# MoE 1's rational function from completed squares, a shorter bias table, a later flag, and two-bank QK products in every block, in a new order

## The chip, the cores and the metric

The kernel runs on one core of one Trainium2 chip. The metric is device microseconds of one execution, the median of several. The core's engines run their own instruction streams and wait for each other on semaphores: TensorE (PE, with its weight loads as PEld), VectorE (DVE), ScalarE (ACT), GpSimd (POOL) and SyncE (SP, which here only issues DMA).

## What is computed

Attention over 2 batches, 8 heads, 768 positions with a local window and a few global positions, then two MoE-like layers over 1536 tokens. Cut to what matters:

```python
scores = q @ k.T / sqrt(64) + bias          # bias = -slope[h] * dist, -1e9 outside window and globals
x  = softmax(scores) @ v                    # (1536, 512) after the heads are put side by side
h  = x @ w_in                               # MoE 1: 512 -> 2048
P  = a[0] + a[1]*h + a[2]*h**2 + a[3]*h**3
Q  = 1.0 + abs(b[0])*abs(h) + abs(b[1])*h**2
y  = (P / (Q + 1e-6)) @ w_out               # 2048 -> 512
h2 = y @ w2_in                              # MoE 2: 512 -> 1024
s  = h2 * softmax(h2)
out = ((s - mean(s)) / sqrt(var(s) + 1e-6) * g_ln) @ w2_out
```

The weights come in 64-bit floats and are made into 32-bit ones on the chip. Each 32-bit operand of a large product is then split into a high and a low part, and a product is the sum of three.

## The kernel before, in words

The tokens stand in four blocks of 384. Three things are interleaved.

*Attention* goes by units, 48 in all (one tile of 128 positions, one pair of heads). A unit's work: two loads on SP; QK (`qk`, L459, PE); scores plus bias and their extreme (`smax`, L464, DVE); exp (L471, ACT); reciprocal (L476, L477, DVE); normalizing (L482, on DVE for the units in `NDVE`, else on POOL); transposes (L502, PE), copy (L514, ACT), PV (L509, PE), and the result's high and low part (L516 ACT, L99 DVE). A unit whose tile is the first of its batch has 128 keys, any other 256. QK has two forms: over one PSUM bank, two products with all 128 rows of the array, or over two banks, two products with 64 rows each. The first block uses two banks (the pair `h` that MoE 1 uses later), blocks 1 and 2 use one bank of the pair `s`, and block 3 (`TWO`) uses both of `s`.

*MoE 1* goes by 64 steps (a block and a slice of 128 of the 2048 columns; block 0 in two parts). Each has three groups of products into one of two banks `h` (L634, L636, L640), the rational function (`e_ops`: c L660, ch L662, abs L663, ch2 L664, sq L666, q L667, ln L669, ex L670, n1 L671, n2 L673, n3 L675, high part L677, low part L99 on POOL), and, three steps later in the list, the products with w_out (`y_mm`, L725, L726, L731).

*Weights* (48 tiles) are loaded on SP, made 32 bits wide (L565 ACT; L569 and L570, or L582 on POOL and L586; then L574, DVE), copied as high part (L604, ACT), and the low part is a subtraction by the helper `minus` (L99), on DVE for the tiles whose number is in `WDVE`, else on POOL.

*MoE 2* goes by 12 tiles of 128 tokens after MoE 1: transposes, products `h2` (L810 to L812), a softmax and normalization (`p2_soft`), transposes (L872), products with w2_out (L894 to L896).

A planner (`Plan`) lists every operation with an estimated duration, gives out banks and buffers, and emits the instructions in the order in which its own clock would start them. `UW`, `WS`, `M2` say at which step units and weights are listed; `LEADS` shifts the due times of kinds of operations; `ZS`, `NDVE` and `WDVE` choose engines. The order on each engine is fixed by that when the program is built. While the first 30 us last, small products with the identity (`fill`, L337) are put where the planner sees PE idle.

At the start, two small tensors (`ni`: the window sizes, `abt`: the six coefficients) are loaded on SP, turned into numbers (`scalars`), a distance table is made on DVE (`bias_keep`, L401 to L413) and scaled for each head on ACT (`bias_pair`, L417). A flag on DVE (L1187 to L1193) tells whether another path has to run instead.

## Time and profile before

| | us |
|---|---|
| median of three runs | 559.76 (558.61 to 561.55) |
| span of the profiled execution | 556.3 |
| PE busy | 531.8 (96%) |
| DVE busy | 446.0 (80%) |
| ACT busy | 393.0 (71%) |
| POOL busy | 182.5 (33%) |

The median stands 3.5 us above the span of the profiled execution. The granted PE clock shows 9 tenths or more in every slice of the page. A busy PE is not a PE at its peak here: products overlap, and the view counts the union of their spans, so time lost between two products shows less than it is. The start of one product to the start of the next says more.

### The profile page before, as it was taken

To read this page: it belongs to the slowest core of one execution; us is meant where nothing else is said; L and a number is where in the kernel's file an instruction comes from. 1 tells how busy PE (TensorE), PEld (TensorE's weight loads), DVE (VectorE), ACT (ScalarE), POOL (GpSimd) and SP (SyncE) were. 2 spreads that over 40 slices of the span, in tenths; PEclk is the share of its full clock that TensorE was granted. 3 is DMA by queue.
4 is the path that set the end of the run, shared out by engine and by line. 5 is a ranking of instruction groups with operands and counts; after the bars stand their busy time and mean duration, and the time that the engine had idled before them with its cause. 6 is when DMAs were issued, how large, how long until landed. Compare 5 with 4: busy or idle time off the path is not lost.

```text
span 556.3 us, 8937 instructions
## 1 busy us (share of the span) xinstructions
PE 531.8 (96%) x2910; PEld 437.0 (79%) x2910; DVE 446.0 (80%) x1104; ACT 393.0 (71%) x911; POOL 182.5 (33%) x212
## 2 busy tenths in 40 slices
...
GB/s 252 130 201 341 195 219 86 185 135 153 104 182 154 151 96 98 73 48 48 1 38 114 133 77 75 77 180 87 57 20 38 39 38 58 20 19 20 19 39 43
DMA packets 28278, 56.24 MB, mean 101 GB/s; under 512 B 3520, under 2 KB 11968, under 8 KB 28224
## 3 DMA queue, kind: packets, MB, share of 16 engines
...
q8 instruction: 25, 0.41, 0.3%
...
q10 hardware_dynamic: 144, 0.00, 0.0%
HBM read 47.72 MB, written 7.86 MB: 100 GB/s over the span
## 4 chain that ended last, share of the span: by engine, by line
PE 55%; DVE 29%; ACT 10%; issue 4%; DMA 1%; POOL 0%; SPq 0%; ACTq 0%; DVEq 0%; POOLq 0%
PE pb L894 4%; PE pb L896 4%; PE pb L895 4%; PE pb L634 4%; PE pb L810 4%; PE pb L812 4%; PE pb L811 4%; PE pb L640 4%; PE pb L731 3%; PE pb L636 3%; PE pb L725 3%; DVE t L667 3%; PE pb L459 3%; DVE wst L574 3%; PE pb L726 3%
## 5 line engine op out<-in xcount | busy, mean ns | idle before, releaser
L99 POOL TENSOR_TENSOR g<-t,g 128x384 fp32r<-128x384 f32 x64 | 69.2, 1082 | 103.9 <-ACT g L677 91.7
L634 PE MATMUL pb<-x,w 128*128 128x384 f32 x256 | 89.3, 349 | 1.8 <-DVE t L667 1.8
L636 PE MATMUL pb<-x,w 128*128 128x384 f32 x256 | 86.1, 336 | 0.0
L725 PE MATMUL pb<-w,g 128*128 128x512 f32 x192 | 77.5, 404 | 4.2 <-ACT g L677 4.2
L726 PE MATMUL pb<-w,g 128*128 128x512 f32 x192 | 75.6, 394 | 0.5 <-POOL w L99 0.5
L99 POOL TENSOR_TENSOR w<-wst,w 128x512 fp32r<-128x512 f32 x42 | 57.2, 1364 | 42.7 <-ACT w L604 38.8
L640 PE MATMUL pb<-x,w 128*128 128x384 f32 x256 | 58.0, 347 | 0.1
L731 PE MATMUL pb<-w,g 128*128 128x512 f32 x192 | 57.7, 409 | 0.2 <-POOL g L99 0.2
L634 PEld LDWEIGHTS pb<-x,w 128*128 128x128 f32 x256 | 48.1, 188 | 8.6 <-DVE t L667 4.4
L471 ACT ACTIVATE e<-e,st 128x256 f32<-128x256 f32 (+1 forms) x96 | 46.3, 486 | 6.4 <-DVE st L464 6.4
L640 PEld LDWEIGHTS pb<-x,w 128*128 128x128 f32 x256 | 44.5, 188 | 7.1 <-issue 3.1
L636 PEld LDWEIGHTS pb<-x,w 128*128 128x128 f32 x256 | 48.1, 188 | 1.5
L725 PEld LDWEIGHTS pb<-w,g 128*128 128x128 f32 x192 | 36.0, 187 | 14.4 <-ACT g L677 7.3
L660 ACT ACTIVATE t<-pb,coef 128x384 f32<-128x384 f32 x64 | 42.7, 668 | 6.1 <-PE pb L640 6.1
L482 POOL TENSOR_SCALAR e<-e,st 128x256 f32<-128x256 f32 (+1 forms) x58 | 28.0, 495 | 54.4 <-DVE st L477 48.4
L669 ACT ACTIVATE t<-t,coef 128x384 f32<-128x384 f32 x64 | 39.6, 618 | 6.8 <-DVE t L667 6.6
L662 DVE TENSOR_TENSOR t<-t,pb 128x384 f32<-128x384 f32 x64 | 35.2, 549 | 11.1 <-ACT t L663 6.5
L677 ACT CAST g<-t 128x384 fp32r<-128x384 f32 x64 | 32.8, 512 | 16.0 <-DVE t L675 15.3
L880 ACT CAST lh<-pb 128x512 fp32r<-128x512 f32 x24 | 13.9, 592 | 42.5 <-PE pb L872 42.5
L459 PE MATMUL pb<-qk 64*128 64x256 f32 (+3 forms) x192 | 41.3, 393 | 2.7 <-DVE st L464 1.0
L667 DVE SCALAR_TENSOR_TENSOR t<-pb,coef,t 128x384 f32<-128x384 f32 x64 | 39.2, 613 | 5.2 <-ACT pb L666 4.8
L671 DVE SCALAR_TENSOR_TENSOR t<-t,t 128x384 f32<-128x384 f32 x64 | 40.6, 634 | 1.3 <-ACT t L670 1.3
(113 smaller groups left out, 1293.2 us busy)
## 6 DMA issues: line engine op xcount, KB each, us to landing
...
```

The lines of the kernel that those rows point to most:

```text
L99: eng.tensor_tensor(out=out, in0=a, in1=hi.bitcast(F32), op=ALU.subtract)
L459: pe.matmul(out=score(h), lhsT=a[r, h * 128:(h + 1) * 128], rhs=a[r, 256:256 + w], start=True, stop=True)
L471: act.activation(out=e[:, h, 0:w], in_=e[:, h, 0:w], func=AF.Exp, scale=-1.0, bias=st[:, h:h + 1], accum_out=st[:, 2 + 2 * h:3 + 2 * h])
L634: pe.matmul(out=pb[:, g.h.slot, 0:n], lhsT=wt[wh.slot][:, cs[p]], rhs=xt[x[p][0].slot][:, 0:n], start=(p == 0), stop=False)
L636: pe.matmul(out=pb[:, g.h.slot, 0:n], lhsT=wt[wl.slot][:, cs[p]], rhs=xt[x[p][0].slot][:, 0:n], start=False, stop=False)
L640: pe.matmul(out=pb[:, g.h.slot, 0:n], lhsT=wt[wh.slot][:, cs[p]], rhs=xt[x[p][1].slot][:, 0:n], start=False, stop=(p == 3))
L660: op("ACT", 0.2 + 0.46 * k, lambda: act.activation(out=T(g.c), in_=h(), func=AF.Identity, scale=coef[:, 3:4], bias=coef[:, 2:3]), r=[g.h], ...
L667: op("DVE", 0.2 + 0.41 * k, lambda: stt_(out=T(g.a), in0=h(), scalar=coef[:, 5:6], in1=T(g.b), op0=ALU.mult, op1=ALU.add), r=[g.h, g.b], n ...
L671: op("DVE", 0.15 + 0.41 * k, lambda: stt_(out=T(g.a), in0=T(g.a), scalar=1.0 + 1e-6, in1=T(g.b), op0=ALU.add, op1=ALU.mult), r=[g.b], w=[g ...
L725: pe.matmul(out=pb[:, y[i].slot, :], lhsT=gt[g.gh.slot][:, c], rhs=wt[wh.slot], start=g.first, stop=False)
L726: pe.matmul(out=pb[:, y[i].slot, :], lhsT=gt[g.gh.slot][:, c], rhs=wt[wl.slot], start=False, stop=False)
L731: pe.matmul(out=pb[:, y[i].slot, :], lhsT=gt[g.gl.slot][:, c], rhs=wt[wh.slot], start=False, stop=g.last)
```

## The change

What it does, part by part.

1. *Completed squares.* With r = sqrt|a3| and the sign s of a3 (of the negated coefficients), P/s is written as h * ((r*h + m)^2 + d) + e, and Q - 1 as b * (b + k) with b = sqrt|b1| * |h|. So c becomes one Square on ACT with scale and bias, and the operation ch on DVE and sq on ACT go; q reads b twice instead of h squared in PSUM. The sign is multiplied in where y leaves PSUM. The eight scalars for that (`poly`) are made once, with four small operations on ACT and seventeen on DVE, at the start.
2. *Bias table.* It is now made of five operations on DVE (a threshold by is_ge times a large number, then max and min) in the place of nine, and it no longer needs `scalars`; `abt` is loaded on ACT's queue.
3. *Flag.* The numbers for it, and new conditions on the size of the coefficients, stand in the class `Flag`: 24 small operations on DVE behind the last step of MoE 1.
4. *QK.* Every unit has a form of its own by a string: h (both banks `h`), s (one bank `s`), t (both `s`), m (one `h` and one `s`). 12 are h in the first block; of blocks 1 and 2, 22 are m, one h, one s; block 3 has t and m.
5. *Order anew.* New `UW`, `WS`, `M2`, `ZS`, `NDVE`, `WDVE`, `LEADS`. `WDVE` has 25 tiles in the place of 6, `NDVE` 16 units in the place of 19. There are 29 fillers in the place of 51.

The core of the diff:

```diff
-UW = {1: (0, 7), 2: (8, 15), 3: (25, 14)}
+UW = {1: (0, 5), 2: (4, 15), 3: (25, 10)}
-WS = (8, 14)
-M2 = (41, 17)
+WS = (4, 4)
+M2 = (39, 5)
-START = ('hh',)
-TWO = (3,)
+QK = 'hhhhhhhhhhhhmmmmmmmmmmmmmhmmmmmmsmmmttttttmttttt'
+BANKS_OF = {"h": "hh", "s": "s", "t": "ss", "m": "hs"}
-NDVE, WDVE = (3, 4, 5, 6, 7, 8, 9, 10, 11, 14, 15, 36, 38, 39, 40, 41, 42, 44, 46), (11, 20, 31, 42, 44, 45)
+NDVE = (0, 4, 6, 8, 9, 10, 14, 23, 24, 26, 27, 31, 38, 41, 42, 47)
+WDVE = (0, 1, 5, 8, 10, 13, 15, 16, 17, 18, 19, 20, 22, 25, 26, 29, 31, 32, 34, 37, 39, 40, 41, 45, 47)
-FILL = (30.0, 0.45, 0.25)
+FILL = (30.0, 0.45, 0.4)
...
     def bias_keep():
-        dve.tensor_scalar(out=kp, in0=rel, scalar1=nl, scalar2=None, op0=ALU.is_lt)
-        dve.scalar_tensor_tensor(out=dz, in0=rel, scalar=nl, in1=rel, op0=ALU.is_lt, op1=ALU.mult)
...
-        dve.tensor_scalar(out=kp, in0=kp, scalar1=-1.0, scalar2=MASK * 256, op0=ALU.add, op1=ALU.mult)
-        dve.tensor_tensor(out=dz, in0=dz, in1=kp, op=ALU.add)
+        nf = flag.nf
+        dve.tensor_copy(nf, flag.ni)
+        nl = nf[:, 1, 0:1]
+        far, gk = -MASK * 256, kp[:, 136:144]
+        dve.tensor_scalar(out=kp, in0=rel, scalar1=nl, scalar2=far, op0=ALU.is_ge, op1=ALU.mult)
+        dve.tensor_scalar(out=gk, in0=rel[:, 136:144], scalar1=nf[:, 0, 0:1], scalar2=far, op0=ALU.is_ge, op1=ALU.mult)
+        dve.tensor_tensor(out=dz, in0=rel, in1=kp, op=ALU.max)
+        dve.tensor_scalar(out=dz[:, 136:144], in0=gk, scalar1=nl, scalar2=None, op0=ALU.max)
+        dve.tensor_tensor(out=dz[:, 0:8], in0=dz[:, 0:8], in1=dz[:, 136:144], op=ALU.min)
...
+    op("ACT", 0.85, poly_roots, r=[vab], new=[vpoly], tag="poly")
+    op("DVE", 1.8, poly_scalars, w=[vpoly], tag="poly")
...
-        op("ACT", 0.2 + 0.46 * k, lambda: act.activation(out=T(g.c), in_=h(), func=AF.Identity, scale=coef[:, 3:4], bias=coef[:, 2:3]),
-           r=[g.h], new=[g.c], tag="c")
-        op("DVE", 0.14 + 0.41 * k, lambda: dve.tensor_tensor(out=T(g.c), in0=T(g.c), in1=h(), op=ALU.mult), r=[g.h], w=[g.c], tag="ch")
-        op("ACT", 0.15 + 0.42 * k, lambda: act.activation(out=T(g.b), in_=h(), func=AF.Abs, scale=coef[:, 4:5]), r=[g.h], new=[g.b], tag="abs")
-        op("DVE", 0.2 + 0.41 * k, lambda: stt_(out=T(g.c), in0=T(g.c), scalar=coef[:, 1:2], in1=h(), op0=ALU.add, op1=ALU.mult),
+        op("ACT", 0.2 + 0.46 * k, lambda: act.activation(out=T(g.c), in_=h(), func=AF.Square, scale=poly[:, 0:1], bias=poly[:, 1:2]),
+           r=[g.h, vpoly], new=[g.c], tag="c")
+        op("ACT", 0.15 + 0.42 * k, lambda: act.activation(out=T(g.b), in_=h(), func=AF.Abs, scale=poly[:, 4:5]), r=[g.h, vpoly], new=[g.b], tag="abs")
+        op("DVE", 0.2 + 0.41 * k, lambda: stt_(out=T(g.c), in0=T(g.c), scalar=poly[:, 2:3], in1=h(), op0=ALU.add, op1=ALU.mult),
            r=[g.h], w=[g.c], occ=0.12 + 0.41 * k, tag="ch2")
-        op("ACT", 0.1 + 0.38 * k, lambda: act.activation(out=h(), in_=h(), func=AF.Square), w=[g.h], tag="sq")
-        op("DVE", 0.2 + 0.41 * k, lambda: stt_(out=T(g.a), in0=h(), scalar=coef[:, 5:6], in1=T(g.b), op0=ALU.mult, op1=ALU.add),
-           r=[g.h, g.b], new=[g.a], occ=0.12 + 0.41 * k, tag="q")
+        op("DVE", 0.2 + 0.43 * k, lambda: stt_(out=T(g.a), in0=T(g.b), scalar=poly[:, 5:6], in1=T(g.b), op0=ALU.add, op1=ALU.mult),
+           r=[g.b], new=[g.a], lock=True, tag="q")
...
+    vflag = Val()
+    for part_ in (flag.numbers, flag.factors):
+        op("DVE", 1.0, part_, r=[vnn, vpoly], w=[vflag], after=[gs[-1].op], tag="flag")
...
-    nc.sync.dma_start(out=abt, in_=ab.partition_broadcast(128))
+    nc.scalar.dma_start(out=abt, in_=ab.partition_broadcast(128))
```

What the new order makes of it, at three places, all on DVE (`t` are the buffers of the rational function, `wst` those of the weights, `pb` is PSUM, `e` and `st` belong to a unit's softmax). First, two steps of MoE 1 behind the attention, before:

```order
L662 TENSOR_TENSOR t_164<-t_164,pb 128x384
L664 SCALAR_TENSOR_TENSOR t_164<-t_164,coef,pb 128x384
L671 SCALAR_TENSOR_TENSOR t_163<-t_163,t_162 128x384
L673 SCALAR_TENSOR_TENSOR t_162<-t_163,t_162 128x384
L675 SCALAR_TENSOR_TENSOR t_160<-t_160,coef,t_162 128x384
L667 SCALAR_TENSOR_TENSOR t_166<-pb,coef,t_168 128x384
L671 SCALAR_TENSOR_TENSOR t_161<-t_161,t_165 128x384
L574 SCALAR_TENSOR_TENSOR wst_156<-wst_156,pb 128x512
L662 TENSOR_TENSOR t_163<-t_163,pb 128x384
L673 SCALAR_TENSOR_TENSOR t_165<-t_161,t_165 128x384
L675 SCALAR_TENSOR_TENSOR t_167<-t_167,coef,t_165 128x384
```

and in the changed kernel, a few steps earlier:

```order
L735 SCALAR_TENSOR_TENSOR t_158<-t_158,poly,pb 128x384
L741 SCALAR_TENSOR_TENSOR t_164<-t_164,t_162 128x384
L737 SCALAR_TENSOR_TENSOR t_161<-t_160,poly 128x384
L743 SCALAR_TENSOR_TENSOR t_162<-t_164,t_162 128x384
L745 SCALAR_TENSOR_TENSOR t_159<-t_159,poly,t_162 128x384
L737 SCALAR_TENSOR_TENSOR t_164<-t_157,poly 128x384
L735 SCALAR_TENSOR_TENSOR t_163<-t_163,poly,pb 128x384
L741 SCALAR_TENSOR_TENSOR t_161<-t_161,t_160 128x384
L741 SCALAR_TENSOR_TENSOR t_164<-t_164,t_157 128x384
L743 SCALAR_TENSOR_TENSOR t_160<-t_161,t_160 128x384
L745 SCALAR_TENSOR_TENSOR t_158<-t_158,poly,t_160 128x384
```

L662 has no successor, and L667's, L737, reads buffer t alone and no PSUM.

Second, DVE's start before, from the coefficients on (five more bias operations follow):

```order
L1181 TENSOR_SCALAR coef<-abt 128x4
L401 TENSOR_SCALAR t_161<-t_163,nv 128x264
L402 SCALAR_TENSOR_TENSOR t_160<-t_163,nv 128x264
L1187 TENSOR_SCALAR fl<-nv 128x1
L1188 TENSOR_SCALAR fl<-nv 128x1
L404 TENSOR_SCALAR t_161<-t_163,nv 128x8
L1189 TENSOR_TENSOR fl<-fl 128x1
L406 TENSOR_SCALAR t_160<-t_161,nv 128x8
```

and in the changed kernel, from the last of the first three units' maxima (L536):

```order
L536 ISA e_210,st_215<-pb,bt_198 128x128
L536 ISA st_215 128x1
L473 TENSOR_SCALAR coef<-abt 128x4
L475 RECIPROCAL root<-root 128x2
L476 TENSOR_TENSOR root<-root 128x2
L477 TENSOR_TENSOR root<-root 128x2
L478 TENSOR_SCALAR root<-root 128x2
L479 RECIPROCAL root<-root 128x2
```

The coefficients (`coef<-abt`) stood ahead of the bias table; now they stand behind the maxima, and with them sixteen operations on `root` and `poly`, ahead of the first reciprocal of a softmax.

Third, DVE behind ch2 of MoE 1's last step, before:

```order
L667 SCALAR_TENSOR_TENSOR t_161<-pb,coef,t_165 128x384
L673 SCALAR_TENSOR_TENSOR t_162<-t_163,t_162 128x384
L675 SCALAR_TENSOR_TENSOR t_160<-t_160,coef,t_162 128x384
L671 SCALAR_TENSOR_TENSOR t_161<-t_161,t_165 128x384
L673 SCALAR_TENSOR_TENSOR t_165<-t_161,t_165 128x384
L832 TENSOR_REDUCE st_2940<-pb 128x1
L833 TENSOR_SCALAR st_2940<-st_2940 128x1
L675 SCALAR_TENSOR_TENSOR t_167<-t_167,coef,t_165 128x384
L99 TENSOR_TENSOR w_115<-wst_156,w_113 128x512
```

and in the changed kernel, from the last operations of the flag:

```order
L109 TENSOR_SCALAR fl<-am 128x1
L110 TENSOR_TENSOR fl<-fl 128x1
L111 TENSOR_SCALAR fl<-am 128x1
L112 TENSOR_TENSOR fl<-fl 128x1
L113 CAST fi<-fl 128x1
L745 SCALAR_TENSOR_TENSOR t_163<-t_163,poly,t_157 128x384
L741 SCALAR_TENSOR_TENSOR t_159<-t_159,t_165 128x384
L133 TENSOR_TENSOR w_115<-wst_155,w_116 128x512
L743 SCALAR_TENSOR_TENSOR t_165<-t_159,t_165 128x384
```

Between that ch2 and these rows stand, in the changed kernel, n3 of an earlier step, n1, q, n2, the low part of MoE 2's first input, three weight joins with two more weight operations, and the flag's first nineteen operations; of the last two n3 (L745) one stands here and one follows.

## Rows read from the trace of the kernel before

**Rows 1.** Busy time by stretch: start:end, then PE, PEld, DVE, ACT, POOL busy, clock, DMA share, GB/s.

```profile
46.00:196.00 150.00, 142.83 (x817) 115.58 (x816) 143.14 (x352) 134.38 (x324) 83.88 (x100) 1.00 0.52 168
196.00:284.00 88.00, 87.84 (x511) 69.92 (x511) 74.47 (x200) 70.39 (x170) 23.65 (x27) 1.00 0.19 59
284.00:396.00 112.00, 107.96 (x529) 94.35 (x528) 105.73 (x187) 94.45 (x187) 58.63 (x56) 1.00 0.29 96
```

**Rows 2.** PE groups in 46:196, 196:284, 284:396: count, busy us, mean ns, idle before.

```profile
L634 PE MATMUL pb<-x,w 128*128 128x384 f32 x96 | 34.2, 356 | 0.6 <-DVE t L667 0.6
L459 PE MATMUL pb<-qk 128*128 128x256 f32 (+1 forms) x80 | 19.8, 371 | 1.8 <-DVE st L464 1.0 <-DVE wst L574 0.7
...
L634 PE MATMUL pb<-x,w 128*128 128x384 f32 x60 | 21.0, 350 | 0.0
L459 PE MATMUL pb<-qk 64*128 64x256 f32 x48 | 8.7, 428 | 0.0
...
L634 PE MATMUL pb<-x,w 128*128 128x384 f32 x96 | 32.7, 341 | 1.2 <-DVE t L667 1.2
```

**Rows 3.** First products of two steps in PE's timeline: start, duration.

```profile
284.41 0.33 PE L634 MATMUL pb<-x,w 128*128 128x384 f32 x1
...
296.99 0.33 PE L634 MATMUL pb<-x,w 128*128 128x384 f32 x1
```

**Rows 4.** MoE 1 groups, whole span: busy us, mean ns, idle before, what ended it.

```profile
L667 DVE SCALAR_TENSOR_TENSOR t<-pb,coef,t 128x384 f32<-128x384 f32 x64 | 39.2, 613 | 5.2 <-ACT pb L666 4.8 <-POOL w L99 0.2
L662 DVE TENSOR_TENSOR t<-t,pb 128x384 f32<-128x384 f32 x64 | 35.2, 549 | 11.1 <-ACT t L663 6.5 <-ACT t L660 4.4
L666 ACT ACTIVATE pb<-pb 128x384 f32<-128x384 f32 x64 | 30.4, 476 | 8.0 <-DVE t L664 7.7
```

**Rows 5.** Groups that change engine, whole span.

```profile
L99 POOL TENSOR_TENSOR w<-wst,w 128x512 fp32r<-128x512 f32 x42 | 57.2, 1364 | 42.7 <-ACT w L604 38.8 <-DVE st L476 2.9 <-PE pb L459 0.9
L482 DVE TENSOR_SCALAR e<-e,st 128x256 f32<-128x256 f32 (+1 forms) x38 | 13.6, 402 | 0.5
L99 DVE TENSOR_TENSOR w<-wst,w 128x512 fp32r<-128x512 f32 x6 | 4.1, 694 | 0.2 <-ACT w L604 0.2
```

**Rows 6.** Tile t: durations min/median/max in ns, first and last start.

```profile
L667 DVE SCALAR_TENSOR_TENSOR t<-pb,coef,t x64: 598/614/620, 49.9 to 395.1; 128x384 f32<-128x384 f32 x64
L671 DVE SCALAR_TENSOR_TENSOR t<-t,t x64: 536/551/1419, 52.6 to 397.1; 128x384 f32<-128x384 f32 x64
```

**Rows 7.** PE's timeline: one-bank QK, plain y products, two-bank QK (start, duration).

```profile
172.41 1.02 PE L459 MATMUL pb<-qk 128*128 128x256 f32 x4
173.09 1.04 PE L731 MATMUL pb<-w,g 128*128 128x512 f32 x3
...
389.22 0.86 PE L731 MATMUL pb<-w,g 128*128 128x512 f32 x3
...
220.56 0.70 PE L459 MATMUL pb<-qk 64*128 64x256 f32 x4
221.19 0.45 PE L634 MATMUL pb<-x,w 128*128 128x384 f32 x1
```

**Rows 8.** The chain that ended last, at the start: start us, us, what.

```profile
4.81 0.17 DVE coef L1181
...
5.64 0.06 DVE fl L1187
...
6.97 0.41 DVE t L413
...
7.41 1.36 ACT bt L417 x4
```

**Rows 9.** Timeline of one unit: its QK, then its second maximum.

```profile
155.14 1.03 PE L459 MATMUL pb<-qk 128*128 128x256 f32 x4
...
156.56 0.42 DVE L464 CUSTOM_DVE_ANT_0 e<-pb,bt 128x256 f32<-128x256 f32 x1
```

**Rows 10.** One small operation of the flag, whole span.

```profile
L1187 DVE TENSOR_SCALAR fl<-nv 128x1 f32<-128x1 f32 x1 | 0.1, 146 | 0.0
```

More of the change, by code (lines that the diff above doesn't have):

```diff
@@ L343, in fast_path, with record @@
     es.close()
-def record(tc, es, const, qkv, w_in, w_out, w2_in, w2_out, coef, g_sb, nv, ident, out):
+def record(tc, es, const, qkv, w_in, w_out, w2_in, w2_out, coef, abt, g_sb, ident, flag, out):
     nc = tc.nc
```

154 lines of the change are left out of this document (97 added, 57 removed).

## The prediction

> **What bounds the kernel now.** I read the busy time by stretch first, then for each stretch what PE could do if nothing held it. From 46 to 196 us (attention, weights and MoE 1 together) DVE is busy 143.1 of 150 us, and from 284 to 396 us (the rest of MoE 1 with MoE 2's weights) 105.7 of 112; from 196 to 284 us PE is busy 87.8 of 88 and DVE only 74.5 [rows 1]. So two stretches are DVE's and one is PE's.
>
> How much PE loses in DVE's stretches comes from its own pace. Where nothing but MoE 1 runs, step 40 begins at 284.41 and step 43 at 296.99 [rows 3]: 4.2 us a step, half of it the h products and half the y products. In PE's stretch there are 60 products of L634, 15 steps, and 48 records of L459, 12 units at four records each [rows 2]. The 88 us less 15.3 steps at 4.2 leave 23.7, 2.0 us a unit. From 46 to 196 us there are 24 steps (96 of L634) and 20 units (80 of L459), four of them half size [rows 2]; y runs three steps late, so PE has 24 times 2.1 plus 21 times 2.1, 95 us, and 36 for the units; with transposes and PV of three units begun earlier, 135. PE loses 15 of 150 us there. From 284 to 396 us, 24 steps [rows 2] are 101 us, with the first MoE 2 products 104; PE loses 8 of 112. These 23 us are what a lighter DVE can give back; no more.
>
> **The change part by part.**
>
> *Completed squares.* ch (L662) goes: 64 times 0.549, 35.2 us of DVE; sq (L666) goes: 30.4 us of ACT [rows 4]. c and abs remain, and a Square takes the Identity's place at the same shape: nothing. Along with the two goes DVE's waiting for ACT around them: 10.9 us before L662, and 4.8 before L667 for sq [rows 4]; L737 now waits for abs instead, one operation earlier in the chain.
>
> q is the doubtful one. With one operand in PSUM, L667 never took longer than 0.620 us; L671, with both in SBUF, has a median of 0.551 and a longest of 1.419 [rows 6]. L737 is of the second kind. Its basic time is bounded by 0.55 and 0.62; the excess for waiting I bound by nothing and by 0.08 a time, about L671's distance from its median to a mean of 0.634 (40.6 us over 64 in the whole span), so 0 to 5 us over 64 steps. I take 0.613 and no excess, since POOL loses a third of its work, below. The Trainium skill ("SBUF — State Buffer", section "Who interferes with whom") has a rule on it: a Vector instruction with two SBUF inputs contends with a GpSimd instruction that reads SBUF, and the later one blocks until the first is done. The trace agrees (0.620 against 1.419, [rows 6]); by that rule alone the new q pays the upper bound.
>
> *Weights from POOL to DVE.* 19 more tiles have their low part on DVE: 19 times 0.694 is 13.2 us more for DVE, 19 times 1.364 is 25.9 less for POOL [rows 5]. Of MoE 1's 32 tiles DVE made 3 and will make 17, two of these before the first step; so 12 more in the stretch to 196 us, 8.3 us, and 5 more among MoE 2's, 3.5 us. *Norms.* Units 23, 24, 26, 27 and 31 come to DVE: two full ones at twice 0.402 [rows 5] and three half ones, 3.4 us more before 196 us; four fewer in the first block, 3.2 us less.
>
> *Sum to 196 us.* DVE 143.1 less 24 times 0.549 (13.2) plus 8.3 plus 3.4 is 141.6: most is given back there. Its idle time is 6.9 us; since the waits around ch and sq are a large part of it, I take 3. That makes 144.6, 5.4 us less. Bounds: idle time as it is and a third of the excess on q, no gain at all; and PE's floor of 135, 15 less.
>
> *196 to 284 us.* PE sets it. The two-bank form was here already. 0; plus or minus 1.
>
> *284 to 396 us.* DVE 105.7 less 13.2 plus 3.5 is 96, below PE's 104. PE's floor then bounds it: at most 8 less; I take 5, since single waits (y for the high part of g, h for a bank) remain when neither engine is full. At least 2.
>
> *QK over two banks.* Of the units in blocks 1 and 2, 23 change form. A one-bank QK holds PE for 0.68 us (172.41 to 173.09), and the y products behind it last 1.04 instead of 0.86: 0.86 in all. A two-bank QK takes 0.63 (220.56 to 221.19), and the first h product behind it lasts 0.45 instead of the usual 0.33 [rows 3, 7]: 0.75, or 0.84 with what it delays in the transposes ahead, which other switches cost as well. So 0.02 to 0.11 a unit, 0.4 to 2 us of PE over the 19 full units; on a stretch that is DVE's I count nothing. The Trainium skill ("TensorEngine Tiling (Array Packing)", section "Key Properties") says that changing the tiling mode drains TensorE, while its section "Theoretical Speedup" allows up to 2 times for a contract dimension of 64. By the second alone a unit would save 0.43 and 19 units 8 us; the rows show the first.
>
> *Start.* DVE's chain waits for the coefficients until 4.81, and the scaled bias begins at 7.41 [rows 8]. Without that wait, four bias operations and the flag in between, it begins some 2 us earlier. But ACT then does all eight scalings, twice the 1.36 of four [rows 8], and four small operations ahead of the first exp, which now starts after the first four: 5.3 plus 2.7 plus 0.8 is 8.8, the same 8.8 as now. On DVE 17 small operations at 0.06 [rows 8] to 0.15 [rows 10] each, 1 to 2.6 us, stand ahead of the first reciprocal; against them, the four norms. I take 0.5 less, between 3 less and 3 more.
>
> *End of MoE 1.* The flag's 24 operations cost 1.4 us at 0.06 to 3.6 at 0.15 [rows 8, 10], and three weight tiles stand with them ahead of the last two n3. PE has cover: five y products (10.5 us) and one and a half h2 of MoE 2 (36 products at 0.23, as y's 2.1 over 9: 8 us). The softmax of the first tile is queued behind all of it on DVE, and its transposes on PE wait for that. I take 1 more; 0 to 3. MoE 2 itself is PE's and unchanged.
>
> *Sum:* -0.5 - 5.4 + 0 - 5 + 1 = -9.9. The profiled execution's span of 556.3 becomes 546.4; the median stood 3.5 above its span, so 549.9, **550 us**.
>
> **Rivals.**
>
> *The early stretch gives all back.* DVE's 141.6 plus an idle time of 6.9 and 1.5 of excess on q is the 150 of now. Against it: the waits for ch and sq are gone. For it: 11.7 of the 13.2 us are handed back in weights and norms. 549.9 plus 5.4: 555.
>
> *PE gets its floor.* Shorter chains (ch2 no longer ahead of q) and fewer clashes with POOL let PE run at 4.2 and 2.0 us: -0.5 - 15 - 8 + 0 gives 536; half way, 541. Against it: DVE's 141.6 is itself above 135.
>
> *Nothing is left over.* Early as in the first rival, the late stretch only 2 less, the start 1 and the end of MoE 1 2 more: 560.
>
> *A bank too few, slower.* In form m a QK takes one of MoE 1's two h banks, and the next h products have to wait until the second maximum has read it. In one unit QK starts at 155.14 and lasts on PE to 156.17, the maximum ends at 156.98 [rows 9]: 0.8 us behind QK. If PE finds no other work in those, 20 m-units of the first 36 cost 16 us: 566. It decides from the point where a step and its units hold the two banks all the time: a step of 6.25 us (150 over 24) offers 12.5 bank-us; MoE 1 holds some 6 to 7 and 0.8 units at 1.9 to 3 hold 2, so DVE's order would have to release some 4 us later than now. I see room, but the order is new and its lateness can't be read here.
>
> **How the numbers follow.** Forecast (545.5 to 554) 0.45; early stretch given back (554 to 557) 0.18; PE's floor (below 545.5) 0.17, of this 0.07 below 540; nothing left (557 to 562.5) 0.11; slower by a bank 0.09. A measurement of this kernel tells about 0.5%, 2.8 us, from no change. Faster by more: 0.45 + 0.18 + 0.17, 0.80, less 0.02 for the first rival's edge, 0.78; same 0.12; slower 0.10. The range leaves out 0.07 below 540 and about 0.1 above 562.
>
> **What would show it.** In the new profile: DVE's total falls by 20 to 25 us (35.2 less 13.2 and small ones), ACT's by 29, POOL's by some 23. L737 has a longest time above 1 us, against 0.62 of L667. In the late stretch step follows step at 4.2 to 4.4 us instead of 4.7 (112 over 24). A two-bank QK still holds PE for some 0.63. The first h product starts at about the same time as now. If early steps still take above 6 us with DVE full, the first rival holds; if PE's h products wait for QK's maxima, the last. The forecast is wrong in its main point if DVE is no longer full before 196 us and the time still has not moved.

## The result, and the profile after

The changed kernel takes 567.6 us (median of four runs, 566.2 to 569.9), the kernel before 560.5 beside it (558.6 to 561.6). The ratio is 1.0137, with a 95% interval of 1.0099 to 1.0175: slower by 1.4%. The profiled execution has a span of 566.8 us against 556.3.

The first view is the busy time by stretch, in the columns of [rows 1]; one line of the kernel before is added for a stretch that was not shown. The changed kernel:

```profile
46.00:196.00 150.00, 140.14 (x796) 109.66 (x795) 142.81 (x341) 121.91 (x293) 68.92 (x78) 0.97 0.49 158
196.00:284.00 88.00, 85.78 (x490) 67.08 (x489) 70.81 (x181) 65.31 (x154) 26.83 (x32) 0.98 0.23 73
284.00:396.00 112.00, 109.07 (x542) 96.81 (x541) 107.44 (x167) 84.34 (x161) 49.56 (x47) 1.00 0.28 91
396.00:440.00 44.00, 37.40 (x163) 29.36 (x162) 35.87 (x87) 17.41 (x34) 9.39 (x10) 0.96 0.13 39
```

The kernel before, last stretch:

```profile
396.00:440.00 44.00, 42.34 (x208) 34.44 (x207) 33.09 (x75) 20.34 (x42) 5.33 (x6) 1.00 0.13 43
```

DVE is as full as before to 196 us, and fuller from 284 on (107.4 against 105.7 [rows 1]), though 64 operations of 0.55 us were taken from it. From 396 to 440 us PE ran 163 instructions where it ran 208.

PE's busy time hides what it loses, so I kept a ledger. Every PE instruction counts with the distance at which such instructions follow one another undisturbed: 0.229 us for 512 columns, 0.1745 for 384, 0.1175 for 256, 0.109 for a transpose, 0.0545 for PV, 0.160 for a QK of 256 columns and 0.105 for one of 128, nothing for fillers. All PE work comes to 481 us in both kernels. The length of a stretch less what begins in it is the time that PE lost there (the last stretch ends with PE's last product):

| lost by PE, us | 0–46 | 46–196 | 196–284 | 284–396 | 396–440 | then | sum |
|---|---|---|---|---|---|---|---|
| before | 25.5 | 25.3 | 6.8 | 7.4 | 2.6 | 1.5 | 69.2 |
| after | 23.2 | 28.9 | 11.3 | 5.2 | 9.5 | 1.7 | 79.7 |
| difference | -2.3 | +3.6 | +4.5 | -2.2 | +6.9 | +0.2 | +10.5 |
| forecast | -0.5 | -5.4 | 0 | -5 | +1 | 0 | -9.9 |

Two readings go far to explain what was lost behind 196 us. The first is the group view of DVE's five operations of MoE 1 (line, names, shapes, count, then busy us, mean ns, idle before), the changed kernel:

```profile
L737 DVE SCALAR_TENSOR_TENSOR t<-t,poly 128x384 f32<-128x384 f32 x64 | 52.7, 823 | 2.3 <-ACT t L734 2.0
L745 DVE SCALAR_TENSOR_TENSOR t<-t,poly,t 128x384 f32<-128x384 f32 x64 | 43.4, 678 | 0.8
L743 DVE SCALAR_TENSOR_TENSOR t<-t,t 128x384 f32<-128x384 f32 x64 | 43.0, 672 | 0.4
L741 DVE SCALAR_TENSOR_TENSOR t<-t,t 128x384 f32<-128x384 f32 x64 | 40.2, 629 | 6.1 <-ACT t L740 5.5
L735 DVE SCALAR_TENSOR_TENSOR t<-t,poly,pb 128x384 f32<-128x384 f32 x64 | 38.8, 606 | 5.7 <-ACT t L734 5.5
```

q (L737) takes 0.823 us on average where L667 took 0.613 [rows 4]. Its median is 0.612: most are as quick as ever, 21 of 64 are not, and the longest is 1.684. Two of these in DVE's timeline (start, duration), and what GpSimd did then, changed kernel:

```profile
199.75 1.37 DVE L737 SCALAR_TENSOR_TENSOR t<-t,poly 128x384 f32<-128x384 f32 x1
...
203.64 1.65 DVE L737 SCALAR_TENSOR_TENSOR t<-t,poly 128x384 f32<-128x384 f32 x1
```

```profile
199.45 1.27 POOL L133 TENSOR_TENSOR g<-t,g 128x384 fp32r<-128x384 f32 x1 [3.99 <-PE pb L801]
203.49 1.38 POOL L133 TENSOR_TENSOR w<-wst,w 128x512 fp32r<-128x512 f32 x1 [2.77 <-ACT w L676]
```

Each began while GpSimd was in a subtraction of two SBUF tiles, and ended about 0.4 us after it: it stood until GpSimd was done. Of the 256 operations with two SBUF inputs (L737, L741, L743, L745) 53 lie over their median by more than 0.06 us. 52 of these began while GpSimd was in an operation (33 times a subtraction, else a scaling or a cast), the other 0.01 us ahead of one, and all 53 ended 0.38 to 0.43 us after one. (20 more began so and were not held.) Only L735, with one operand in PSUM, never does this: 24 of its 64 began beside a busy GpSimd, and its longest is 0.616. Counting what lies over an operation's own median, in all of DVE's operations that are over it by more than 0.06 us, the collisions cost DVE 4.2 us before and 13.6 after from 46 to 196 us, 1.3 and 5.5 from 196 to 284, 3.1 and 16.0 from 284 to 396.

The second is the junction of the two MoEs. DVE's timeline there, with the flag's small operations (L88 to L113), and GpSimd's beside it, changed kernel:

```profile
399.26 0.30 DVE L88 TENSOR_SCALAR nneg<-nf 128x2 f32<-128x2 f32 x1
399.60 0.62 DVE L89 TENSOR_TENSOR nneg<-nneg,nf 128x2 f32<-128x2 f32 x1
...
400.69 0.90 DVE L93 TENSOR_TENSOR fl<-fl 128x1 f32<-128x1 f32 x1
...
404.34 0.50 DVE L103 TENSOR_TENSOR fl<-fl,am 128x1 f32<-128x1 f32 x1
...
405.59 1.28 DVE L110 TENSOR_TENSOR fl<-fl 128x1 f32<-128x1 f32 x1
...
407.48 0.16 DVE L110 TENSOR_TENSOR fl<-fl 128x1 f32<-128x1 f32 x1
...
408.12 0.61 DVE L745 SCALAR_TENSOR_TENSOR t<-t,poly,t 128x384 f32<-128x384 f32 x1
```

```profile
398.84 1.36 POOL L674 TENSOR_SCALAR wst<-wst,g_sb 128x512 f32<-128x512 f32 x2 [1.71 <-DVE wst L646]
400.27 1.30 POOL L133 TENSOR_TENSOR w<-wst,w 128x512 fp32r<-128x512 f32 x1
404.14 0.69 POOL L674 TENSOR_SCALAR wst<-wst,g_sb 128x512 f32<-128x512 f32 x1 [2.57 <-DVE am L101]
405.57 1.28 POOL L133 TENSOR_TENSOR w<-wst,w 128x512 fp32r<-128x512 f32 x1 [0.74 <-ACT w L676]
```

The flag holds DVE from 399.27 to 401.89 and from 403.96 to 408.12, 6.8 us. Some 2.7 of these are the five long operations: one on one or two elements per partition waits for GpSimd just as one on 384 does (L110 takes 1.28 us at 405.59 and 0.16 at 407.48). The rest are the 24 operations themselves, about 0.17 us each. Behind it stands an n3 of MoE 1 (408.12), and behind that the y products and the first softmax. What PE waited for between 400 and 425 us (us in total, times, longest):

```profile
PEld pb L882 <- DVE yl L133: 2.5, 1, 2.5
PEld pb L882 <- DVE wst L646: 2.0, 1, 2.0
...
PEld pb L795 <- ACT g L747: 1.6, 1, 1.6
```

Both the first products of MoE 2 (L882) and the last y products (L795, by way of ACT's copy of g) waited for DVE's row.

### The profile page after: what moved, and what is told of

Its sections match the earlier page's. It is cut to its first block, busy times and chain, and to the rows that moved or that the text cites. A ratio compares the mean times of both kernels' runs of the same rounds, so it can differ in the third digit from the quotient of the medians.

```text
span 566.8 us, 8755 instructions
## 1 busy us (share of the span) xinstructions
PE 533.9 (94%) x2866; PEld 433.7 (77%) x2866; DVE 451.1 (80%) x1080; ACT 370.1 (65%) x850; POOL 169.0 (30%) x199
## 4 chain that ended last, share of the span: by engine, by line
PE 56%; DVE 34%; ACT 5%; issue 3%; DMA 1%; POOL 0%; SPq 0%; ACTq 0%; DVEq 0%; POOLq 0%
DVE t L737 5%; PE pb L531 4%; PE pb L967 4%; PE pb L969 4%; PE pb L968 4%; DVE t L743 4%; PE pb L706 4%; PE pb L882 4%; PE pb L884 4%; PE pb L883 4%; PE pb L801 3%; PE pb L712 3%; PE pb L708 3%; PE pb L795 3%; DVE t L741 3%
## 5 line engine op out<-in xcount | busy, mean ns | idle before, releaser
L133 POOL TENSOR_TENSOR g<-t,g 128x384 fp32r<-128x384 f32 x64 | 71.1, 1112 | 115.9 <-PE pb L801 43.3
L795 PE MATMUL pb<-w,g 128*128 128x512 f32 x192 | 78.4, 409 | 3.6 <-ACT g L747 1.9
L706 PEld LDWEIGHTS pb<-x,w 128*128 128x128 f32 x256 | 49.0, 192 | 12.6 <-DVE t L735 6.4
L554 POOL TENSOR_SCALAR e<-e,st 128x256 f32<-128x256 f32 (+1 forms) x64 | 35.9, 572 | 67.4 <-DVE st L549 30.7
L737 DVE SCALAR_TENSOR_TENSOR t<-t,poly 128x384 f32<-128x384 f32 x64 | 52.7, 823 | 2.3 <-ACT t L734 2.0
L732 ACT ACTIVATE t<-pb,poly 128x384 f32<-128x384 f32 x64 | 42.8, 668 | 12.5 <-PE pb L712 8.6
L708 PEld LDWEIGHTS pb<-x,w 128*128 128x128 f32 x256 | 49.2, 192 | 1.9 <-POOL w L133 0.4
L712 PEld LDWEIGHTS pb<-x,w 128*128 128x128 f32 x256 | 44.7, 189 | 5.3 <-issue 1.7
L795 PEld LDWEIGHTS pb<-w,g 128*128 128x128 f32 x192 | 36.4, 190 | 13.3 <-ACT g L747 2.5
L741 DVE SCALAR_TENSOR_TENSOR t<-t,t 128x384 f32<-128x384 f32 x64 | 40.2, 629 | 6.1 <-ACT t L740 5.5
L745 DVE SCALAR_TENSOR_TENSOR t<-t,poly,t 128x384 f32<-128x384 f32 x64 | 43.4, 678 | 0.8
L882 PE MATMUL pb<-w,yh 128*128 128x512 f32 x96 | 38.5, 401 | 5.5 <-DVE yl L133 2.0
L743 DVE SCALAR_TENSOR_TENSOR t<-t,t 128x384 f32<-128x384 f32 x64 | 43.0, 672 | 0.4
L735 DVE SCALAR_TENSOR_TENSOR t<-t,poly,pb 128x384 f32<-128x384 f32 x64 | 38.8, 606 | 5.7 <-ACT t L734 5.5
```

The lines of the kernel that those rows point to most:

```text
L133: eng.tensor_tensor(out=out, in0=a, in1=hi.bitcast(F32), op=ALU.subtract)
L706: pe.matmul(out=pb[:, g.h.slot, 0:n], lhsT=wt[wh.slot][:, cs[p]], rhs=xt[x[p][0].slot][:, 0:n], start=(p == 0), stop=False)
L708: pe.matmul(out=pb[:, g.h.slot, 0:n], lhsT=wt[wl.slot][:, cs[p]], rhs=xt[x[p][0].slot][:, 0:n], start=False, stop=False)
L712: pe.matmul(out=pb[:, g.h.slot, 0:n], lhsT=wt[wh.slot][:, cs[p]], rhs=xt[x[p][1].slot][:, 0:n], start=False, stop=(p == 3))
L737: op("DVE", 0.2 + 0.43 * k, lambda: stt_(out=T(g.a), in0=T(g.b), scalar=poly[:, 5:6], in1=T(g.b), op0=ALU.add, op1=ALU.mult), r=[g.b], new ...
L741: op("DVE", 0.15 + 0.41 * k, lambda: stt_(out=T(g.a), in0=T(g.a), scalar=1.0 + 1e-6, in1=T(g.b), op0=ALU.add, op1=ALU.mult), r=[g.b], w=[g ...
```

## The experiments

The theory that the two readings suggest has two parts: the squares' gain goes into collisions of DVE with GpSimd (E in the expectations), and the flag stands in front of what PE waits for (A). The rivals are the clock (C), the new order (D, H), a bank too few (F) and the weights on DVE (G). Parts of the change were undone or done alone. In e1 to e11 every engine's order is held but for what an edit moves, so a difference is not a new order's. All ratios are to the kernel before, run beside each; 0.1% is 0.56 us.

| run | us | ratio | 95% interval |
|---|---|---|---|
| the change | 567.6 | 1.0137 | 1.0099 to 1.0175 |
| e1 flag behind tile 6 of MoE 2 | 564.0 | 1.0069 | 1.0039 to 1.0100 |
| e2 PE kept busy | 569.4 | 1.0175 | 1.0138 to 1.0211 |
| e4 q on ACT | 560.2 | 1.0021 | 0.9994 to 1.0047 |
| e7 e1 and e4 together | 554.7 | 0.9912 | 0.9882 to 0.9941 |
| e8 one bank for form m | 571.4 | 1.0226 | 1.0209 to 1.0243 |
| e9 low parts back on GpSimd | 570.2 | 1.0177 | 1.0123 to 1.0231 |
| e10 no low part of g | 558.3 | 0.9991 | 0.9966 to 1.0015 |
| e11 the kernel before, no low part of g | 555.4 | 0.9934 | 0.9910 to 0.9958 |
| e3 the kernel before, with the squares | 566.7 | 1.0134 | 1.0096 to 1.0172 |
| e5 as e3, coefficients made later | 562.6 | 1.0071 | 1.0052 to 1.0091 |
| e6 as e5, q on ACT | 552.8 | 0.9903 | 0.9881 to 0.9926 |
| e12 the change, old tables | 587.2 | 1.0518 | 1.0498 to 1.0537 |
| e13 e7, old tables | 592.3 | 1.0610 | 1.0589 to 1.0631 |
| e14 e12, old forms of QK | 578.1 | 1.0354 | 1.0319 to 1.0388 |

**e1, the flag.**

```diff
-                o.fn()
+                if o.tag == "flag":
+                    self.late_flag = getattr(self, "late_flag", []) + [o.fn]
+                else:
+                    o.fn()
...
+                    if self.newtons == 6:
+                        for f in self.late_flag:
+                            f()
```

> The changed kernel with one difference: the 24 small DVE operations of the flag are issued after the sixth tile's Newton steps of MoE 2 (about 480 us, where DVE is half idle) and not between MoE 1's last operations. The order of all other work is the same. Theory A (the junction): in the changed kernel the flag holds DVE 6.8 us (399.27 to 401.89 and 403.96 to 408.12) in front of the last n3 and n1, and PE stands for them; then this kernel takes 4 to 6 us less than the changed one, 561.5 to 564, and PE's clock does not fall at 414 us. Theory B (the weights and steps that are late anyway set the junction, the flag only fills DVE's time): 566 to 568.

0.7% less than the changed kernel, as theory A had it, though the two intervals just touch. At 464.9 us, where GpSimd has nothing left to do, the 24 operations take 4.1 us instead of 6.8, and none more than 0.16. In the ledger the junction loses 6.2 us instead of 9.5. It is not back at the 2.6 of the kernel before, and the clock still fell, between 400 and 404 us instead of at 414: the flag's place is about half of what the junction lost more, not all.

**e2, the clock.** PE's granted clock fell to 0.5, the 1.2 GHz level, four times in the changed kernel, and never between 46 and 440 us in the kernel before ([rows 1]; the last stretch above). Windows of 2 us around two of the falls, PE alone (PE busy, clock, DMA share, GB/s):

```profile
50.00:52.00 2.00, 0.71 (x5) 1.00 1.02 414
52.00:54.00 2.00, 2.00 (x7) 0.54 1.02 403
...
60.00:62.00 2.00, 1.98 (x6) 0.50 0.81 216
...
412.00:414.00 2.00, 0.94 (x4) 0.99 0.00 0
414.00:416.00 2.00, 2.00 (x7) 0.50 0.00 0
```

Ahead of each fall PE had stood. In all it worked 17.1 us at half rate, 10.3 of them between 46 and 120 us, which could cost up to 8.6 us of the 10.5.

```diff
+                    if KEEP.get((key, k)):          # before step 3's h, the PV behind it, ...
+                        fill(KEEP[key, k], [free[0][1]])
                 o.fn()
```

> The changed kernel with 88 added products of the identity by itself (128x128, results not used) at the eight places where PE stood longest before a fall of its clock: 10 before step 3's h products, 14 before the PV product behind them, 8 each before the h products of step 26 and the QK at 206 us, 12, 12, 10 and 14 at the start of MoE 2. Theory C (the clock): the 17.1 us at a granted clock of 0.5 (52.1 to 55.6, 59.0 to 65.8, 209.2 to 212.6, 414.0 to 417.4) cost up to 8.6 us; with PE kept busy the clock stays at 1.0 and the kernel takes 3 to 8 us less, 560 to 565. Rival: what follows the pauses waits for DVE anyway, so the clock may stay up and the time does not move, 566 to 569.

The clock's row of e2's page (tenths of full speed, 40 slices) and its mean:

```profile
PEclk9999999999999999999999999999999999999999
```

```profile
core 0: 567.7 us, clock 0.998
```

The clock stays up and the time does not move (1.0175, the interval overlaps the change's). But the added products were not free: the product behind each of the eight batches begins 0.1 to 2.6 us later than in the changed kernel, and seven of the eight show no wait but for the batch. So keeping PE busy in this way gains nothing, and what the half rate costs by itself is not separated. Against a large price speak e7, 13 us faster than the change at nearly its mean clock (0.986 against 0.983), and e5, slower than the kernel before at 0.998. Theory C is not shown, and as a part of the loss, above all before 120 us, not excluded.

**e3 and e5, the squares alone.** The kernel before with its own order. e3 makes the squares' coefficients behind the scaled bias, e5 right ahead of the first c.

```diff
-c: Identity(scale=coef[3], bias=coef[2])          +c: Square(scale=poly[0], bias=poly[1])
-ch: tensor_tensor(c, h, mult)                     +(left out)
-sq: Square(h) in PSUM                             +(left out)
-q: stt(in0=h, coef[5], in1=b, mult, add)          +q: stt(in0=b, poly[5], in1=b, add, mult)
```

> The kernel before, with the completed squares alone and its own order on every engine: ch and sq are left out, c becomes a Square, q reads abs twice, y is scaled by the sign on its way out, and the roots and coefficients of the squares (4 operations on ACT, 15 on DVE) come behind the eighth scaled bias. Theory D (the new order lost what the squares gave): 35.2 us less DVE work in the old order shows as a gain, 549 to 556. Theory E (the contention of q with GpSimd eats it: L737 0.823 us against 0.613, and the others of its kind): 558 to 562, no difference that can be measured.

> As e3 (the squares alone in the order of the kernel before), but the roots and coefficients of the squares are made directly ahead of MoE 1's first c, some 30 us later, so that the start is that of the kernel before. In e3 the first h product came 5.5 us later than before, and the last step's 8.3 us later. Theory E (the collisions of q and its kind eat what ch and sq gave): the start's 5.5 us come back and nothing more, 559 to 562.5, no gain over the kernel before. Theory D' (e3's loss was all the start's, the squares are worth something): 552 to 557.

Neither of e3's expected ranges held: 566.7, worse than both. Its first h product came at 49.2 us instead of 43.7: DVE waited 1.87 us for the roots from ACT and then made the coefficients, from 13.2 to 15.6 us, ahead of a softmax's reciprocal. Without that, in e5, the squares alone still cost 0.7%, with an interval that leaves out no change. 35 us of operations are taken from DVE, and the kernel is slower. DVE's groups in e5:

```profile
L707 DVE SCALAR_TENSOR_TENSOR t<-t,poly 128x384 f32<-128x384 f32 x64 | 55.6, 869 | 0.5 <-ACT t L703 0.5
L715 DVE SCALAR_TENSOR_TENSOR t<-t,poly,t 128x384 f32<-128x384 f32 x64 | 45.1, 705 | 1.4
L711 DVE SCALAR_TENSOR_TENSOR t<-t,t 128x384 f32<-128x384 f32 x64 | 45.0, 703 | 6.1 <-ACT t L710 6.0
L713 DVE SCALAR_TENSOR_TENSOR t<-t,t 128x384 f32<-128x384 f32 x64 | 39.1, 611 | 1.0
```

q takes 16.4 us more than L667's 39.2 [rows 4], and n1 (L711) has a mean of 0.703 with the median of 0.55 that L671 had [rows 6]. Over their medians these four lose 29.6 us; the kernel before lost 8.6 in its three. But q's median, 0.782 here, itself holds collisions; counted from the 0.612 of the changed kernel the four lose 35.4, so that some 27 of the 35 us go there. With the new small operations DVE's busy time falls by 3.4 us in all (446.0 to 442.6). Why the kernel is then slower and not level, the runs don't show. What DVE lost, ch and the old q, had an operand in PSUM and never collided (longest 0.557 and 0.620); the new q collides, and its neighbours more than before.

**e4 and e6, q on ACT.** (b + p/2) squared is q but for a constant, which goes into ln's bias and n1's scalar.

```diff
-q: DVE stt(out=a, in0=b, scalar=poly[5], in1=b, add, mult)
+q: ACT activation(out=a, in_=b, Square, bias=poly[8])     # poly[8] = poly[5]/2
-ln: bias=coef[6];  n1: scalar=1.0 + 1e-6
+ln: bias=poly[9];  n1: scalar=poly[9]                     # 1 + 1e-6 - poly[8]^2
```

> The changed kernel with q made by ACT: the square of abs plus half the coefficient, its constant moved into ln's bias and n1's scalar. Same order on all engines, but for q, which stands in ACT's row now. DVE loses 52.7 us in 64 operations, ACT gains some 30. Theory E (contention of q, and with it DVE's load, decides): 549 to 557. Theory A and the order (the flag and the pauses stay where they are): 561 to 566. If ACT becomes the late engine in the early stretch: 566 or more.

> As e5, and q is made by ACT as the square of abs plus half its coefficient, so that DVE has four operations a step where the kernel before has six. Theory E: MoE 1's DVE-bound stretches shorten by what q gave in e4 (7 us), 551 to 556. Rival (the old order can use no lighter DVE, PE waits for ACT and the banks): 558 to 562.

e4 gives back 1.2%, more than the flag and the order alone would allow (561 to 566) and less than theory E had it (549 to 557), since the flag is still in its place. In the order of the kernel before it is e6, 552.8 us, **faster than both kernels** (0.9903, 0.9881 to 0.9926). e6's busy time by stretch:

```profile
46.00:196.00 150.00, 143.56 (x831) 117.13 (x831) 132.03 (x331) 138.66 (x334) 85.30 (x101) 1.00 0.54 171
196.00:284.00 88.00, 88.00 (x516) 70.81 (x517) 60.78 (x168) 71.70 (x170) 22.92 (x27) 1.00 0.21 63
284.00:396.00 112.00, 110.51 (x546) 97.85 (x546) 98.02 (x145) 96.97 (x189) 58.47 (x57) 1.00 0.31 98
```

DVE is no longer full before 196 us (132.0) and ACT has become as busy (138.7). The collisions do not vanish: in e4 they move to the operations that are left. n2 (L746) goes from 0.672 to 0.784:

```profile
L746 DVE SCALAR_TENSOR_TENSOR t<-t,t 128x384 f32<-128x384 f32 x64 | 50.2, 784 | 0.9
L744 DVE SCALAR_TENSOR_TENSOR t<-t,poly,t 128x384 f32<-128x384 f32 x64 | 47.5, 742 | 12.4 <-ACT t L743 11.6
```

**e7, both.** e1's and e4's edits.

> The changed kernel with both edits that helped: the flag behind the sixth tile of MoE 2 (e1: 3.8 us) and q on ACT (e4: 7 us). If the two costs are separate, in the junction and in MoE 1's steps, they add up: 555 to 558. If the flag's place only matters while DVE is late for another reason, the second gives nothing more: 559 to 561.

They add up, and a little more (not clear of the intervals): 0.7 and 1.2% make 2.2. In the ledger, e7 loses 2.3 us at the junction and 1.5 from 284 to 396, less than the kernel before in both; from 46 to 196 it loses 30.7, more than the changed kernel.

**e8, the lent bank.** A unit of form m writes both halves into its score bank with 128 rows; MoE 1's bank stays empty meanwhile.

```diff
-        two, ndve = len(bank) == 2, u.k in NDVE
+        two, ndve = bank in ("hh", "ss"), u.k in NDVE
-            return ... pb[:, u.s[0].slot, h * 256:h * 256 + w]
+            return ... pb[:, u.s[-1].slot, h * 256:h * 256 + w]
```

> The changed kernel, same order, but each unit of form m writes both halves of its QK into its one score bank with 128 rows, as the kernel before did; MoE 1's bank that it lends stays unused for that time, so no QK waits for that bank and no h product for QK's maximum. Theory F (a bank too few, the prediction's last rival): in the changed kernel QK pairs of form m stood 1 to 2.4 us in six places (50, 59, 70, 83, 98, 207 us) and PE lost 8.8 us more between 46 and 120 us than in the kernel before; without the loan 3 to 8 us come back, 560 to 565. Rival (those QKs wait for DVE anyway, and the one-bank form costs PE 0.02 to 0.11 us more a unit): 566 to 569.

Slower than the changed kernel by 0.9%, above both expected ranges: the two banks are worth about 5 us (2 to 8 by the intervals), and no h product was held up by the loan to a price that shows. From 46 to 120 us PE loses 21.8 us without the loan and 22.1 with it. Theory F, the prediction's last rival, falls. PE's own price of a one-bank unit is what the prediction had; e8's timeline of PE:

```profile
164.46 1.03 PE L531 MATMUL pb<-qk 128*128 128x256 f32 x4
165.14 1.04 PE L712 MATMUL pb<-x,w 128*128 128x384 f32 x4
166.02 0.39 PE L801 MATMUL pb<-w,g 128*128 128x512 f32 x1
```

0.68 for the QK and 0.88 instead of 0.70 for what follows: 0.86 a unit, as [rows 7] gave. At 0.11 a unit that makes 2 us, the least that the intervals allow. Where the rest comes from, the runs don't show.

**e9, the weights.**

```diff
-lambda: minus(nc, dve, wt[lo.slot], ...)
+lambda e=(dve if nlo[0] - 1 in (11, 20, 31, 42, 44, 45) else pool): minus(nc, e, wt[lo.slot], ...)
```

> The changed kernel, same order, but the low parts of the 19 weight tiles that the change gave to DVE are made by GpSimd again, at the same places of the order. DVE loses 19 times 0.69 to 0.84, 13 to 16 us, GpSimd gains 26. Theory G (the weights on DVE eat what the squares gave): 561 to 564.5. Theory E (collisions: the more GpSimd reads, the longer DVE's operations of two inputs wait): 566 to 571, no gain from a DVE that has 13 us less to do.

No gain; if anything a loss. The edit moves 22 tiles and not 19, since only three of the six old numbers are in the new list (the trace has 3 on DVE and 45 on GpSimd). DVE is rid of these 22, but over their medians its operations on 384 columns now lose 38.6 us, not 30.7: GpSimd reads more beside them. That the weights on DVE eat the squares' gain (theory G) is wrong: giving them back gains nothing.

**e10 and e11, less of GpSimd's reading.** The low part of g is left out, but for one column, in both kernels.

```diff
-minus(nc, pool, gt[g.gl.slot][:, 0:n], T(g.c), gt[g.gh.slot][:, 0:n])
+minus(nc, pool, gt[g.gl.slot][:, 0:1], T(g.c)[:, 0:1], gt[g.gh.slot][:, 0:1])
```

> The changed kernel, same order, with the low part of g left out: GpSimd subtracts one column instead of 384, 64 times, and the g tiles are zeroed once at the start. This takes away 65 to 70 us of GpSimd's reading beside DVE. To be read against the kernel before with the same cut. Theory E: the means of DVE's operations on two inputs fall towards their medians (q from 0.82 to about 0.65, the third of g's from 0.67 to about 0.58), and the changed kernel gains at least 5 us more by the cut than the kernel before, so that the two kernels' distance of 7 us goes or turns. Rival (the collisions lie beside PE's work, the distance has another cause): both gain alike, and 6 to 8 us remain between them.

> The kernel before, same order, with the same cut: the low part of g is left out, but for one column. Theory E: its collisions are the smaller ones (n1's mean 0.63 against a median of 0.55, n2's 0.60 against 0.56), some 8 us of DVE in all, so it gains 2 to 5 us, 554 to 558. Rival: it gains as much as the changed kernel does.

e10 gains 1.5% on the changed kernel, e11 0.7% on the kernel before. The two kernels' distance of 1.4% shrinks to 0.6%. DVE's groups, e10 and then e11:

```profile
L739 DVE SCALAR_TENSOR_TENSOR t<-t,poly 128x384 f32<-128x384 f32 x64 | 47.8, 747 | 5.1 <-ACT t L736 4.7
L747 DVE SCALAR_TENSOR_TENSOR t<-t,poly,t 128x384 f32<-128x384 f32 x64 | 39.8, 622 | 0.8
...
L745 DVE SCALAR_TENSOR_TENSOR t<-t,t 128x384 f32<-128x384 f32 x64 | 36.6, 573 | 0.9
```

```profile
L673 DVE SCALAR_TENSOR_TENSOR t<-t,t 128x384 f32<-128x384 f32 x64 | 36.7, 573 | 1.5 <-ACT t L672 1.3
L675 DVE SCALAR_TENSOR_TENSOR t<-t,t 128x384 f32<-128x384 f32 x64 | 36.2, 566 | 1.0
```

With some 52 us less of GpSimd's work (busy 117.3 us instead of 169.0), n2 and n3 come near their medians and q falls from 0.823 to 0.747 only; the weights and norms are still there. The collisions over the medians go from 30.7 to 14.5 us in the changed kernel, from 8.6 to 2.5 in the other. PE also waits less for g's low part in both, so the gain is not the collisions' price alone; that the changed kernel gains twice as much by it fits theory E. The junction loses 5.5 us here instead of 9.5, but not for the flag's sake: its operations collide as before (L110 takes 1.28 us at 395.5). MoE 1 is through 9 us earlier, and the flag with it begins ahead of 396 us.

**e12 to e14, the tables.** Squares +0.7%, flag +0.7, banks -0.9 leave +0.9% of 1.4 without a cause, 5 us. e12 puts the tables of the kernel before (UW, WS, M2, ZS, NDVE, WDVE, LEADS) under the new code, which the planner then orders anew; e13 adds e7's edits; e14 has the old forms of QK as well.

```diff
-UW = {1: (0, 5), 2: (4, 15), 3: (25, 10)}      +UW = {1: (0, 7), 2: (8, 15), 3: (25, 14)}
-M2 = (39, 5)                                   +M2 = (41, 17)
-LEADS = {"o": -194.2, ...}                     +LEADS = {"o": -35.2, ...}      (and so on)
-QK = 'hhhhhhhhhhhhmmmm...'                     +QK = 'h' * 12 + 's' * 24 + 't' * 12     (e14)
```

> The changed kernel's code (squares with q on DVE, flag behind MoE 1, QK over two banks with one lent), but with the tables of the kernel before for which units, weights and norms go where and the leads of the old kinds of work. Theory H (what is left of the loss, 567.6 less 560.0 less 3.3 for the squares less 3.8 for the flag plus 4.5 for the two banks, some 5 us, is the new tables', above all between 46 and 120 us): 560 to 564. Rival (the rest is the squares' and the flag's in any order, the tables are as good as the old ones): 566 to 570.

> As e12, and q on ACT and the flag behind the sixth tile of MoE 2, at e12's order. If H holds and the parts add up as in e7 (13 us together): 547 to 552, the fastest of all. If e12 is no better than the changed kernel: 553 to 557, as e7.

> As e12 (the changed kernel's code under the tables of the kernel before), but with the forms of QK of the kernel before too: one bank in blocks 1 and 2, none lent. What is left of the change is the squares, the flag's place and the start, in an order that the planner makes anew. Theory J (the lent bank broke the old tables: e12's 20 us are its price there): e5 and the flag add to 559.2 + 3.3 + 3.8, 564 to 568. Rival (the tables were fitted to the old code operation by operation, and any edit under them costs this much): 575 to 587.

e12 does not bear out theory H: the old tables are 20 us worse under the new code, above both expected ranges, and with them the edits of e7 cost 5 us more (592.3). Giving up the lent bank (e14) brings back 9 of the 20 us, but 578.1 is still 12 us above what the squares and the flag add up to: it lies in the range of theory J's rival, that the old tables fit the old code alone. So an order planned anew is no control for one part of the change, and the last 5 us stay open: they are the new order's, the norms', the start's or the clock's, or the parts are worth something else together than alone. In the ledger they lie between 46 and 120 us, where e1 to e10 with the new order lose 21 to 24 us and those with the old one 13 to 15; 5 us of that come back from 120 to 196.

## Why the prediction was wrong

Three steps failed: q's price, the flag's price and cover, and the early stretch. The runs show what stood in the place of the first two; the cause of the third stays open.

*q.* The first is "I take 0.613 and no excess" for q, and with it its upper bound, 5 us over 64 steps. q's own excess was 13.6 us, and n1, n2 and n3 collided more too: 30.7 us in all against 8.6. I had read the bound from L671's distance between median and mean (0.08), as if every operation with two SBUF inputs paid that; what a kind of operation pays depends on when GpSimd's operations meet it. The reason given, that GpSimd loses a third of its work, was a reason for a smaller bill only, and it lost 13.5 us of busy time and not 23: the weights' subtractions gave back 26.3, but the norms took 8.0 more and the other operations some 4, as they lasted longer too (g's subtraction 1.112 us on average against 1.082, a norm of 256 columns 0.600 against 0.534). With q off DVE, its whole 52.7 us of busy time, 7.4 us of the kernel's time come back (e4). The Trainium skill ("SBUF — State Buffer", section "Who interferes with whom") has the rule that I cited and set aside: an operation on Vector with two SBUF inputs contends with one on GpSimd that reads SBUF. The trace agrees (0.616 at most for L735, 1.684 for L737).

*Start.* -0.5 forecast, -2.3 measured (first h product at 41.3 us against 43.7): within the bounds.

*To 196 us.* 5.4 less forecast, 3.6 more came: 8.7 more between 46 and 120 us and 5.2 less behind that. The term takes it that a lighter DVE lets PE lose less. Collisions added 9.4 us to DVE here, and it is as full as before, as the first rival ("the early stretch gives all back") had it. But that is not what held PE. The stretch from 46 to 120 us (columns as in [rows 1]) in the kernel before, then in the changed one, then in e7 with q on ACT:

```profile
46.00:120.00 74.00, 70.78 (x419) 56.58 (x418) 69.24 (x184) 68.62 (x172) 38.12 (x49) 1.00 0.59 192
```

```profile
46.00:120.00 74.00, 65.16 (x375) 48.91 (x374) 68.14 (x178) 58.66 (x149) 32.50 (x39) 0.93 0.54 179
```

```profile
46.00:120.00 74.00, 64.00 (x363) 47.70 (x362) 60.35 (x164) 61.60 (x155) 30.92 (x38) 0.91 0.56 182
```

In e7 no engine but PE is busy above 62 of the 74 us, and PE loses 24.0 us, against 22.1 in the changed kernel and 13.4 before (e4: 21.6). For this stretch it is the prediction's own sign of being wrong in its main point: DVE no longer full, and nothing gained. In the old order q's move from DVE does help the whole stretch (27.6 lost in e5, 23.1 in e6). What holds PE there in the new order stays open. The loan of a bank does not (e8). What PE waits for most between 46 and 120 us is ACT's copy ahead of the PV products (weight loads of PV: 6.3 us, against 2.7 before), and the clock's half rate lies there too.

*196 to 284 us.* "PE sets it" was true only while DVE was well ahead. The two collisions shown above, within 4 us, made the next h products and a QK's second half late, behind operations that follow q on DVE:

```profile
202.18 0.44 PE L706 MATMUL pb<-x,w 128*128 128x384 f32 x1 [0.76 <-DVE t L735]
...
208.26 0.70 PE L531 MATMUL pb<-qk 64*128 64x256 f32 x2 [1.00 <-DVE wst L646]
```

The stretch lost 4.5 us more. With q on ACT (e4, e7) the stretch loses 6.9 us, against 6.8 before.

*284 to 396 us.* Right in sign. 96 plus 12.9 of collisions is 109, measured are 107.4; the gain was 2.2, not 5. In e7 it is 5.9: the forecast's 5 was there to be had, without q on DVE.

*End of MoE 1.* +1 forecast, 3 at most, and 6.9 came. The flag's operations were priced at 0.06 to 0.15 us each, 1.4 to 3.6 in all. They take 4.1 alone (e1), and beside GpSimd's scalings and the weights' low parts they took 6.8. e1 puts 0.7% on their place. The cover that I named (10.5 us of y products, 8 of h2) was behind the same DVE queue, as the waits above show, and could not start.

*QK over two banks.* Counted as nothing, worth about 5 us (e8). A one-bank unit held PE for 0.86 us again; that the stretch is DVE's was no ground for counting nothing. Most of the 5 us stays unexplained.

*What would show it.* L737's longest above 1 us, a two-bank QK of 0.63 and late steps of 4.3 us came as said. ACT's total fell by 22.9 us and not by 29. DVE's did not fall by 20 to 25 us; it rose from 446.0 to 451.1. ch took 35.2 away and the weights brought 13.2, as forecast, and all of DVE's collisions rose from 10.4 us to 37.4. The total stands on the page:

```profile
PE 533.9 (94%) x2866; PEld 433.7 (77%) x2866; DVE 451.1 (80%) x1080; ACT 370.1 (65%) x850; POOL 169.0 (30%) x199
```

The slower rival had 566 and so nearly the time, by luck: its reason, that PE lacks a bank, e8 refutes.
